# Attention of a fused attention and two-layer kernel: from half arrays to 64x64 quarters of TensorE

## The chip, the core and the metric

The kernel runs on one core of one Trainium2 chip. The metric is the device time of one launch in microseconds (us), the median of several runs; lower is better.

## What is computed

Four sequences of 768 tokens go through a retention layer of 8 heads (64 features a head) and then through two feed-forward layers:

```
state = gamma[h] * state + k_t v_t^T            # per head, 64x64
y_t   = scale * q_t state
x     = y as [3072, 512]
x     = leaky_relu(x @ w_in) @ w_out            # 512 -> 2048 -> 512, slope 0.01
out   = elu(x @ w_in2) @ w_out2                 # 512 -> 2048 -> 512
```

The weights arrive as float64 (the kernel reads their words and converts them). The retention is computed in chunks of 128 tokens: inside a chunk, scores `k q^T` are multiplied by a mask that holds the decay and the causal triangle, and the masked scores multiply `v`; a state of 64x64 for each head carries what came before from chunk to chunk.

## The kernel before, in words

There are 24 chunks of 128 tokens (6 for each sequence). `kkv[c]` holds a chunk: k and q feature-major (64 features of a head in one half of the partitions, two heads of a pair `a` one above the other), k and v token-major (128 tokens in the partitions). A chunk takes these products on TensorE (PE), all in float32, which the trace records as two instructions for each `matmul` of the program:

- scores (L240): eight products with 64 rows of contraction, 128 stationary columns and 128 moving columns. The two heads of a pair use the two halves of the rows, so two run side by side.
- inner products (L250, early L379): eight products, 128 rows of contraction (the tokens), 64 stationary columns of v, 128 moving columns of the masked scores; two halves of the columns side by side.
- state products (L254, early L360): eight, 128 rows, 64 stationary columns of k, 64 moving columns of v; two side by side. Not in the last chunk of a sequence.
- crossed products (L258, early L383): eight, 64 rows, 64 stationary columns of the state, 128 moving columns of q; all four quarters of the array side by side. Not in the first chunk of a sequence.

VectorE (DVE) multiplies the scores by the mask (L289, early L352, 128x1024), ScalarE (ACT) copies the result out, GpSimd (POOL) multiplies k and q by decay tables (`prep_k`, `prep_q`, `early_k`).

The feed-forward products are float32 split in high and low parts, 128x128 stationary and 512 moving columns: L196 and L557 in the first stage, L866, L875, L1188 and L1300 later.

Order of the work. Chunks 0 to 7 (`EC = 8`) run at the start, alone on PE, while their k, q, v and the first weights are loaded by one queue of SyncE (SP): `early_tasks` lists the order on PE by hand (`score`, `rest`, `accumulate`), and `AHEAD` says behind which chunk's load each of the first pieces of weights is loaded. The weights are converted from float64 piece by piece on DVE and ACT (L99 to L164; a piece is done when the split of L164 is), and the first step of the feed-forward layer needs piece 0. Chunks 8 to 12 are put between the steps of the feed-forward layer in `scheduled`, chunks 13 to 23 in the loop at L1345; there scores and outputs are two tasks with feed-forward products between them. The order on PE is fixed; the other engines' order is set by a planner in the program (L697 to L731, L1395 to L1437) from costs and due times that each task is given, and each engine then runs its own instructions in that order. From about chunk 13 on, DVE also makes combinations of the weights (`enc_tasks`, L974 to L988), which are stored through two buffers `fe` and one buffer `te`, and loaded again later.

In the early chunks the state of a sequence is summed in one PSUM tile `total` (tag z), and ACT copies it out scaled (`early_copy`).

Of the kernel before, what the change touches and what calls it, by code (L numbers as in the profile page):

```python
# [31 lines left out]
DM, DFF = 512, 2048  # L32
# [16 lines left out]
TABS = H + NP + EARLY + C  # L49
# [7 lines left out]
def body(ctx: ExitStack, tc: tile.TileContext, kkv, w1, w2, tabs, rows, out):  # L57
# [147 lines left out]
    with ExitStack() as actx:  # L205
# [6 lines left out]
        tab = ab.tile([P, H * C + NP * C + H + NP], F32, tag="tab", name="tab")  # L212
        mask = tab[:, : H * C].rearrange("p (r t) -> p r t", r=2)
        qtab = tab[:, H * C : H * C + NP * C]
        small = tab[:, H * C + NP * C :]
# [19 lines left out]

        def scores(c, sc):

            for a in range(NP):
                for r in range(2):
                    nc.tensor.matmul(sc[:, r, pair(a)], kv[c][half(r), 0, pair(a)], kv[c][half(r), 1, pair(a)],  # L240
                                     start=True, stop=True, skip_group_check=True)

        def outputs(c, o, t):

            cb = c % NCB
            places = [(i, k, 2 * i + k, r) for i in range(2) for k in range(2) for r in range(2)]
            by_column = [(i, k, 2 * i + k, x ^ k) for i in range(2) for k in range(2) for x in range(2)]
            for i, k, a, r in by_column:
                v = kv[c][:, 3, a * C + r * D : a * C + (r + 1) * D]
                nc.tensor.matmul(o[half(r ^ k), k, pair(i)], v, t[:, r, pair(a)], start=(i == 0), stop=True, skip_group_check=True)  # L250
            if cb < NCB - 1:
                for i, k, a, r in places:
                    hs = slice(a * C + r * D, a * C + (r + 1) * D)
                    nc.tensor.matmul(o[half(r), k, 2 * C + i * D : 2 * C + (i + 1) * D], kv[c][:, 2, hs], kv[c][:, 3, hs],  # L254
                                     start=False, stop=True, skip_group_check=True)
            if cb:
                for i, k, a, r in places:
                    nc.tensor.matmul(o[half(r ^ k), k, pair(i)], st[half(r), 2 * k + i, :], kv[c][half(r), 1, pair(a)],  # L258
                                     start=False, stop=True, skip_group_check=True)
# [19 lines left out]
        def chunk_tasks(c, task, pe_task, x_bank, t, x, needs, takes=None, uses=None, after=None):  # L279
# [8 lines left out]
            pe_task(("sc", c), 1.16, needs["sc"], lambda: scores(c, x_bank()), **more("sc"))  # L288
            task(("pt", c), "V", 1.22, [("sc", c)] + needs["pt"], lambda: nc.vector.tensor_tensor(t(), x_bank(), mask, ALU.mult), **more("pt"))  # L289
# [8 lines left out]
            pe_task(("o", c), 1.1 + (0.64 if cb < NCB - 1 else 0.0) + (0.67 if cb else 0.0), ready, lambda: outputs(c, x_bank(), t()), **more("o"))  # L298
# [12 lines left out]
        causal = early[:, EARLY : EARLY + C]  # L311
# [12 lines left out]
        total = aps.tile([P, NP, D], F32, tag="z", name="total")  # L324
# [25 lines left out]
        def early_masked(c):  # L350
            pt[c] = spare[:, :2, :] if c % 2 else ptile
            nc.vector.tensor_tensor(pt[c], scs.pop(c), mask, ALU.mult)  # L352

        def early_state(c):
            for i in range(2):
                for k in range(2):
                    for r in range(2):
                        a = 2 * i + k
                        hs = slice(a * C + r * D, a * C + (r + 1) * D)
                        nc.tensor.matmul(total[half(r), 2 * k + i, :], kv[c][:, 2, hs], kv[c][:, 3, hs],  # L360
                                         start=(c % NCB == 0 and i == k == 0), stop=True, skip_group_check=True)

        def early_copy(c):
            n = behind(c)[1]
            t = sts[(c + 1) % 2]
            if n == 0:
                nc.scalar.copy(t, total)
            else:
                for a in range(NP):
                    x = (NCB - 1) * H + (n - 1) * NP + a  # L370
                    nc.scalar.activation(t[:, a, :], total[:, a, :], AF.Copy, scale=early[:, x : x + 1])

        def early_out(c):
# [3 lines left out]
            for i, k, a, r in [(i, k, 2 * i + k, x ^ k) for i in range(2) for k in range(2) for x in range(2)]:  # L377
                v = kv[c][:, 3, a * C + r * D : a * C + (r + 1) * D]
                nc.tensor.matmul(o[half(r ^ k), k, pair(i)], v, t[:, r, pair(a)], start=(i == 0), stop=True, skip_group_check=True)  # L379

        def early_inner(c):
            for i, k, a, r in [(i, k, 2 * i + k, r) for i in range(2) for k in range(2) for r in range(2)]:
                nc.tensor.matmul(os_[c][half(r ^ k), k, pair(i)], sts[c % 2][half(r), 2 * k + i, :], kv[c][half(r), 1, pair(a)],  # L383
                                 start=False, stop=True, skip_group_check=True)
# [10 lines left out]
        def early_tasks(task, pe):  # L395
# [8 lines left out]
            def tab_load():  # L404
                nc.sync.dma_start(out=small, in_=tabs[:, : H + NP])
                nc.sync.dma_start(out=early[:, : EARLY + C], in_=tabs[:, H + NP :])
# [26 lines left out]
            def score(c):  # L433
                pe_task(("sc", c), 1.16, [loaded(c, 0), room(("pt", c))], lambda: early_score(c))
                task(("pt", c), "V", 1.22, [("sc", c), ("mask",), ("o", c - 2) if c > 1 else None], lambda: early_masked(c))
# [5 lines left out]
            def rest(c):  # L441
                with_state = c % NCB < NCB - 1
                pe_task(("o", c), 1.09, [("pt", c), room(("xlo", c))], lambda: early_out(c))
                if c % NCB:
                    pe_task(("i", c), 0.67, [("pq", c), ("stc", c - 1)], lambda: early_inner(c))
# [3 lines left out]
            def accumulate(c):  # L449
# [3 lines left out]
                pe_task(("S", c), 0.63, [("pk", c), loaded(c, 1), before], lambda: early_state(c))  # L453
# [5 lines left out]
            def mask_products():  # L459
                t = scs["mask"] = aps.tile([P, 2, BLK], F32, tag="x", name="mask")  # L460
                for r in range(2):
                    nc.tensor.matmul(t[:, r, :], few[:, r * P : (r + 1) * P], few[:, 2 * P + r * BLK : 2 * P + (r + 1) * BLK], start=True, stop=True)

            def make_mask():
                y = scs.pop("mask").rearrange("p r (a t) -> p (r a) t", a=NP)
                nc.vector.tensor_tensor(mask.rearrange("p r (a t) -> p (r a) t", a=NP), y,
                                        causal.unsqueeze(1).to_broadcast([P, H, C]), ALU.mult)
# [7 lines left out]
            task(("mask",), "V", 1.22, [("mm",), ("tab", 0)], make_mask)  # L475
# [17 lines left out]

# [948 lines left out]
def _tables():  # L1442
# [4 lines left out]
    ktab = gamma[:, None] ** (C - 1.0 - t)  # L1447
    tab = np.zeros((P, TABS), np.float32)
    tab[:, :H] = ktab.T
# [70 lines left out]
```

## Time and profile before

| what | value |
|---|---|
| median of 3 runs | 1097.19 us (1096.94 to 1097.47) |
| profiled execution, its own time | 1096.89 us |
| its span, first to last instruction | 1095.1 us |
| mean granted TensorE clock | 0.999 |
| PE busy | 99% of the span |
| DVE, ACT, POOL busy | 75%, 61%, 5% |

The profile has the busy share of every engine over the span, the groups of instructions by line, the waits, a timeline of each engine, and the chain of work that ended last. Durations are in us or ns; a matmul's end is modelled, so that neighbouring matmuls overlap in the timeline and their starts are what counts.

### The profile page before, as it was taken

To read this page: it belongs to the slowest core of one execution; us is meant where nothing else is said; L and a number is where in the kernel's file an instruction comes from. 1 tells how busy PE (TensorE), PEld (TensorE's weight loads), DVE (VectorE), ACT (ScalarE), POOL (GpSimd) and SP (SyncE) were. 2 spreads that over 40 slices of the span, in tenths; PEclk is the share of its full clock that TensorE was granted. 3 is DMA by queue.
4 is the path that set the end of the run, shared out by engine and by line. 5 is a ranking of instruction groups with operands and counts; after the bars stand their busy time and mean duration, and the time that the engine had idled before them with its cause. 6 is when DMAs were issued, how large, how long until landed. Compare 5 with 4: busy or idle time off the path is not lost.

```text
span 1095.1 us, 16119 instructions
## 1 busy us (share of the span) xinstructions
PE 1080.8 (99%) x5785; PEld 884.4 (81%) x5785; DVE 822.6 (75%) x1298; ACT 673.2 (61%) x1128; POOL 54.2 (5%) x45
## 2 busy tenths in 40 slices
PE   9999999899999999999999999999999999999998
PEld 6878877677888888888878888888888888888886
DVE  5999975885756766566675569989988989879932
ACT  4675643333656655455654478788888778878831
POOL 4110112131000000000000000000000000000000
PEclk9999999999999999999999999999999999999999
DMA  9964547999887876676867966786676776674373
GB/s 358 423 263 168 177 150 231 312 315 294 280 270 252 280 239 210 217 229 217 292 215 254 310 209 197 253 285 193 200 232 185 263 225 189 205 224 152 123 231 109
DMA packets 115592, 258.17 MB, mean 236 GB/s; under 512 B 10924, under 2 KB 41772, under 8 KB 111160
## 3 DMA queue, kind: packets, MB, share of 16 engines
q1 hardware_dynamic: 115488, 257.04, 71.4%
q8 instruction: 46, 0.75, 0.3%
q14 instruction: 34, 0.28, 0.1%
q10 hardware_dynamic: 24, 0.09, 0.0%
HBM read 200.47 MB, written 56.62 MB: 235 GB/s over the span
## 4 chain that ended last, share of the span: by engine, by line
PE 86%; DVE 6%; DMA 6%; ACT 1%; issue 0%; SPq 0%; DVEq 0%; ACTq 0%
PE y L1300 40%; PE x L1188 15%; PE h L1188 10%; PE px L1188 10%; PE y L557 4%; PE h L196 3%; DMA kv<-in_kkv 2%; DMA w1enc<-te 1%; PE y L875 1%; PE x L250 1%; DMA xscr<-xs 1%; PE x L240 1%; DMA xscr<-pt 1%; DVE te L987 1%; DMA w<-xscr 1%; PE px L866 1%
## 5 line engine op out<-in xcount | busy, mean ns | idle before, releaser
L1300 PE MATMUL y<-w,ghi 128*128 128x512 f32 x768 | 236.7, 389 | 0.0
L1300 PE MATMUL y<-ghi,w 128*128 128x512 f32 x512 | 177.1, 389 | 0.0
L1300 PEld LDWEIGHTS y<-w,ghi 128*128 128x128 f32 x768 | 144.0, 188 | 30.2 <-ACT gk L889 0.2
L1300 PE MATMUL y<-w,glo 128*128 128x512 f32 x384 | 149.4, 389 | 0.0
L1300 PEld LDWEIGHTS y<-ghi,w 128*128 128x128 f32 x512 | 96.1, 188 | 20.0
L1188 PE MATMUL x<-w 128*128 128x512 f32 x432 | 109.8, 389 | 0.1
L1300 PE MATMUL y<-glo,w 128*128 128x512 f32 x256 | 99.6, 389 | 0.0
L1320 DVE TENSOR_TENSOR glo<-gk,ghi 128x512 fp32r<-128x512 f32 x89 | 61.4, 689 | 50.6 <-ACT ghi L1317 49.8
L1188 PEld LDWEIGHTS x<-w 128*128 128x128 f32 x432 | 81.0, 188 | 17.3 <-DVE gf L1222 0.5
L1317 ACT CAST ghi<-gk 128x512 fp32r<-128x512 f32 x89 | 55.4, 622 | 52.9 <-PE y L1300 52.0
L1300 PEld LDWEIGHTS y<-w,glo 128*128 128x128 f32 x384 | 72.1, 188 | 15.0
L1222 DVE TENSOR_TENSOR gk<-gk,x 128x512 f32<-128x512 f32 x64 | 44.0, 687 | 43.4 <-PE x L1188 36.7
L1269 DVE SCALAR_TENSOR_TENSOR a<-nt,a 128x512 f32<-128x512 f32 x96 | 65.9, 686 | 11.5 <-ACT nt L1265 11.2
L1277 DVE SCALAR_TENSOR_TENSOR nt<-a,nt 128x512 f32<-128x512 f32 x96 | 66.3, 691 | 2.7
L1273 DVE SCALAR_TENSOR_TENSOR nt<-nt 128x512 f32<-128x512 f32 x96 | 65.8, 685 | 0.0
L1257 ACT ACTIVATE nt<-nt 128x512 f32<-128x512 f32 x96 | 60.8, 633 | 2.9 <-DVE gk L1281 0.4
L1261 ACT ACTIVATE a<-nt 128x512 f32<-128x512 f32 x96 | 60.8, 633 | 2.1
L1188 PE MATMUL px<-w 128*128 128x512 f32 x240 | 60.9, 389 | 0.0
L1188 PE MATMUL h<-w 128*128 128x512 f32 x240 | 60.9, 389 | 0.0
L1265 ACT ACTIVATE nt<-nt 128x512 f32<-128x512 f32 x96 | 59.5, 621 | 0.0
L1300 PEld LDWEIGHTS y<-glo,w 128*128 128x128 f32 x256 | 48.0, 188 | 10.0
L196 PE MATMUL h<-xhi,w 128*128 128x512 f32 x168 | 55.3, 394 | 0.0
(202 smaller groups left out, 2061.9 us busy)
## 6 DMA issues: line engine op xcount, KB each, us to landing
w<-w2scr SPq DMA_DIRECT2D x96, 512.0 KB, 3.9
w<-w1scr SPq DMA_DIRECT2D x168, 256.0 KB, 3.3
w<-w1enc SPq DMA_DIRECT2D x112, 256.0 KB, 3.8
kv<-in_kkv SPq DMA_DIRECT2D x22, 1024.0 KB, 7.1
raw<-in_w SPq DMA_DIRECT2D x40, 512.0 KB, 5.1
raw<-in_w SPq DMA_DIRECT2D x12, 1024.0 KB, 13.5
w2scr<-raw SPq DMA_DIRECT2D x16, 512.0 KB, 4.6
w1enc<-w SPq DMA_DIRECT2D x24, 256.0 KB, 3.9
```

Of the source, the lines that this page charges most:

```text
L196: nc.tensor.matmul(h, a, x, start=(n == 0), stop=(n == 3 * KD - 1))
L1188: nc.tensor.matmul(to, a, x, start=(first and z == 0), stop=(z == 5), skip_group_check=True)
L1222: task(("s", *hk[b]), "V", 0.7, [("c", *hk[b])] + deps, lambda: tt(at(t), at(t), bank[name], add), use=[t])
L1257: nc.scalar.activation(t, n, AF.Tanh, scale=-0.5)
L1261: nc.scalar.activation(a, t, AF.Copy, bias=-0.5, scale=0.5)
L1265: nc.scalar.activation(n, n, AF.Exp, scale=-1.0)
L1269: nc.vector.scalar_tensor_tensor(out=a, in0=n, scalar=1.0, in1=a, op0=ALU.add, op1=ALU.mult)
L1273: nc.vector.scalar_tensor_tensor(out=t, in0=n, scalar=1.0, in1=t, op0=ALU.add, op1=ALU.mult)
L1277: nc.vector.scalar_tensor_tensor(out=t, in0=a, scalar=2.0, in1=t, op0=ALU.add, op1=ALU.mult)
L1300: nc.tensor.matmul(ybank[d], a, x, start=(first and n == 0), stop=(last and n == 2))
L1317: task(hi, "A", 0.62, [made_by, last_hi[0]], lambda h=h, hi=hi: nc.scalar.copy(at(hi), at(h)), use=[h], take=("ghi", hi))
L1320: task(lo, "V", 0.7, [hi], lambda h=h, hi=hi, lo=lo: tt(at(lo), at(h), f32(at(hi)), sub), use=[h, hi], take=("glo", lo))
```

## The change

The token-major k and v are laid out anew on the host: the 128 tokens of a chunk are split in two halves of 64 (`x` = 0, 1), and a head's two halves stand below each other in the columns, in one half of the partitions (`k`, the head's pair modulo 2). All of a chunk's products now use 64x64 quarters of the array, and the four heads of `HEADS` go to the four quarters:

- Scores: 16 products in place of 8. For the first 64 keys all 128 queries are computed, for the second 64 keys only the second 64 queries: the block above the diagonal is left out. The mask and its table have 2 x 384 columns (TRI = 192 for each head) in place of 2 x 512.
- Inner products: 16, with 128 or 64 moving columns. State products: 16, 64 rows of contraction, 64 moving columns, the two halves of the tokens accumulated.
- Crossed products: each split in two of 32 stationary columns (16 in place of 8).
- Early chunks: `total` becomes two tiles, in the PSUM banks of tags h and z; ACT's unscaled copy becomes two instructions. The order on PE is new, and `AHEAD` is (3, 7, 7, 7) in place of (3, 4, 5, 7): pieces 1 to 3 of the weights are loaded after all eight chunks.
- The costs given to the planner are changed.

```diff
-        AHEAD = (3, 4, 5, 7)
+        AHEAD = (3, 7, 7, 7)
...
         def scores(c, sc):
-            for a in range(NP):
-                for r in range(2):
-                    nc.tensor.matmul(sc[:, r, pair(a)], kv[c][half(r), 0, pair(a)], kv[c][half(r), 1, pair(a)],
-                                     start=True, stop=True, skip_group_check=True)
+            for i in range(2):
+                for x in range(2):
+                    for k, r in HEADS:
+                        a = (2 * i + k) * C + x * HC
+                        nc.tensor.matmul(sc[half(k), r, cells(i, x)], kv[c][half(r), 0, a : a + HC], kv[c][half(r), 1, a : a + C - x * HC],
+                                         start=True, stop=True, skip_group_check=True)
+
+        def inner(c, o, t):
+            for i in range(2):
+                for x in range(2):
+                    for k, r in HEADS:
+                        nc.tensor.matmul(o[half(r ^ k), k, i * C + x * HC : (i + 1) * C], kv[c][half(k), 3, block(i, r, x)], t[half(k), r, cells(i, x)],
+                                         start=(i == x == 0), stop=True, skip_group_check=True)
+
+        def products(c, to, fresh):
+            for i in range(2):
+                for x in range(2):
+                    for k, r in HEADS:
+                        nc.tensor.matmul(to(k, r, i), kv[c][half(k), 2, block(i, r, x)], kv[c][half(k), 3, block(i, r, x)],
+                                         start=(fresh and i == x == 0), stop=True, skip_group_check=True)
+
+        def crossed(c, o, s, n):
+            for i in range(2):
+                for z in range(D // n):
+                    for k, r in HEADS:
+                        p = (r ^ k) * D + z * n
+                        nc.tensor.matmul(o[p : p + n, k, pair(i)], s[half(r), 2 * k + i, z * n : (z + 1) * n], kv[c][half(r), 1, pair(2 * i + k)],
+                                         start=False, stop=True, skip_group_check=True)
...
+        def masked(t, sc):
+            nc.vector.tensor_tensor(t[:, :, : 2 * TRI], sc[:, :, : 2 * TRI], mask, ALU.mult)
...
             score(0)
             for k, n in enumerate(WARM[1]):
                 pe_task(("warm", 0, k), n * 0.002, [("qtab",)], lambda n=n: warm(n))
-            rest(0)
-            for k, n in enumerate(WARM[2]):
-                pe_task(("warm", 1, k), n * 0.002, [], lambda n=n: warm(n))
             accumulate(0)
             score(1)
-            accumulate(1)
-            for c in range(1, EC):
-                if c + 1 < EC:
-                    score(c + 1)
-                rest(c)
-                if c + 1 < EC:
+            for c in range(EC):
+                if c < EC - 1:
+                    rest(c)
+                split = c + 1 < EC and (c + 1) % NCB < NCB - 1
+                if split:
                     accumulate(c + 1)
+                if c + 2 < EC and not split:
+                    score(c + 2)
+                if c == EC - 2:
+                    rest(EC - 1)
+                across(c)
+                if c + 2 < EC and split:
+                    score(c + 2)
```

`rest` now holds the inner products alone and `across` the crossed products and the copies to `xhi` and `xlo`.

## Rows read from the trace of the kernel before

**Rows 1.** The page, parts 1 and 2: busy time, and DMA in 40 slices.

```profile
PE 1080.8 (99%) x5785; PEld 884.4 (81%) x5785; DVE 822.6 (75%) x1298; ACT 673.2 (61%) x1128; POOL 54.2 (5%) x45
...
DMA  9964547999887876676867966786676776674373
```

**Rows 2.** The waits of PE, whole span: us in total, times, longest.

```profile
PE x L250 <- DVE pt L289: 4.6, 5, 2.2
PE sc L240 <- DMA kv<-in_kkv: 1.3, 2, 0.8
```

**Rows 3.** The chain that ended last: start, us, what; first and last of eleven pieces.

```profile
161.08 8.13 DMA xscr<-pt
...
234.53 1.91 DVE w L1123
```

**Rows 4.** Timeline of PE, one later chunk (97 to 106 us): start, us, instruction, count.

```profile
97.16 1.16 PE L240 MATMUL x<-kv 64*128 64x128 f32 x16
98.25 0.50 PE L196 MATMUL h<-xhi,w 128*128 128x512 f32 x1
...
102.56 1.09 PE L250 MATMUL x<-pt,kv 128*64 128x128 f32 x16
103.49 0.63 PE L254 MATMUL x<-kv 128*64 128x64 f32 x16
104.05 0.67 PE L258 MATMUL x<-kv,stg 64*64 64x128 f32 x16
104.65 0.50 PE L557 MATMUL y<-ghi,w 128*128 128x512 f32 x1
```

**Rows 5.** The same timeline, cut off at 102.84, 102.95, 103.60, 104.08 and 104.25 us.

```profile
102.56 0.55 PE L250 MATMUL x<-pt,kv 128*64 128x128 f32 x6
...
102.56 0.66 PE L250 MATMUL x<-pt,kv 128*64 128x128 f32 x8
...
103.49 0.28 PE L254 MATMUL x<-kv 128*64 128x64 f32 x4
...
104.05 0.34 PE L258 MATMUL x<-kv,stg 64*64 64x128 f32 x4
...
104.05 0.45 PE L258 MATMUL x<-kv,stg 64*64 64x128 f32 x8
```

**Rows 6.** Timeline of all engines, end of the early chunks (27 to 37 us).

```profile
28.43 1.16 PE L240 MATMUL sc<-kv 64*128 64x128 f32 x16 [0.84 <-DMA kv<-in_kkv]
...
30.77 0.28 DVE L99 TENSOR_SCALAR s<-e 128x512 uint16<-128x512 uint16 x1
30.81 1.14 POOL L348 TENSOR_TENSOR kv<-kv,early 128x512 f32<-128x512 f32 x1 [1.40 <-DMA kv<-in_kkv]
...
32.96 1.23 DVE L352 TENSOR_TENSOR early<-sc,tab 128x1024 f32<-128x1024 f32 x1
...
34.76 0.68 DVE L391 TENSOR_TENSOR xlo<-o,xhi 128x512 fp32r<-128x512 f32 x1
...
35.87 0.50 PE L196 MATMUL h<-xhi,w 128*128 128x512 f32 x1
```

**Rows 7.** Timeline of PE, scores of two early chunks that follow one another.

```profile
21.48 1.16 PE L240 MATMUL sc<-kv 64*128 64x128 f32 x16
...
24.80 1.16 PE L240 MATMUL sc<-kv 64*128 64x128 f32 x16
```

**Rows 8.** Stretches: length, busy PE, PEld, DVE, ACT, POOL, then PEclk, DMA share, GB/s.

```profile
18.00:36.00 18.00, 17.16 (x329) 14.53 (x326) 16.58 (x24) 10.15 (x26) 8.93 (x8) 1.00 1.02 421
36.00:97.00 61.00, 60.10 (x264) 49.26 (x264) 58.95 (x97) 43.12 (x61) 2.94 (x2) 1.00 0.77 301
```

**Rows 9.** Timelines of DVE and PE: a weight piece's last operation, its first use.

```profile
88.08 1.22 DVE L164 TENSOR_TENSOR w<-f,w 128x1024 fp32r<-128x1024 f32 x1
...
91.63 0.39 PE L196 MATMUL h<-xhi,w 128*128 128x512 f32 x1
```

**Rows 10.** The page, part 6: issues, KB each, median us to landing.

```profile
kv<-in_kkv SPq DMA_DIRECT2D x22, 1024.0 KB, 7.1
```

More of the change, by code (lines that the diff above doesn't have):

```diff
@@ L211, in body @@
         st, sg = stg[:, 0], stg[:, 1]
[L212 to L215, printed above, removed]
+        tab = ab.tile([P, 3 * BLK + H + NP], F32, tag="tab", name="tab")
+        mask = tab[:, : 4 * TRI].rearrange("p (r t) -> p r t", r=2)
+        qtab = tab[:, 2 * BLK : 3 * BLK]
+        small = tab[:, 3 * BLK :]
         ktab, gtab = small[:, :H], small[:, H:]
@@ L247, in outputs @@
[L247 to L250, printed above, removed]
+            inner(c, o, t)
             if cb < NCB - 1:
[L252 to L255, printed above, removed]
+                products(c, lambda k, r, i: o[half(r), k, 2 * C + i * D : 2 * C + (i + 1) * D], False)
@@ L256, in outputs @@
             if cb:
-                for i, k, a, r in places:
-                    nc.tensor.matmul(o[half(r ^ k), k, pair(i)], st[half(r), 2 * k + i, :], kv[c][half(r), 1, pair(a)],
-                                     start=False, stop=True, skip_group_check=True)
+                crossed(c, o, st, D // 2)
+        def masked(t, sc):
+            nc.vector.tensor_tensor(t[:, :, : 2 * TRI], sc[:, :, : 2 * TRI], mask, ALU.mult)
         def rows_out(c, x):
@@ L286, in more @@
                 return dict(([("use", uses[n])] if n in uses else []) + ([("take", takes[n])] if n in takes else []))
-            pe_task(("sc", c), 1.16, needs["sc"], lambda: scores(c, x_bank()), **more("sc"))
-            task(("pt", c), "V", 1.22, [("sc", c)] + needs["pt"], lambda: nc.vector.tensor_tensor(t(), x_bank(), mask, ALU.mult), **more("pt"))
+            pe_task(("sc", c), 0.93, needs["sc"], lambda: scores(c, x_bank()), **more("sc"))
+            task(("pt", c), "V", 0.95, [("sc", c)] + needs["pt"], lambda: masked(t(), x_bank()), **more("pt"))
             ready = [("pt", c)]
@@ L297, in chunk_tasks @@
             yield
[L298 removed]
+            pe_task(("o", c), 0.88 + (0.5 if cb < NCB - 1 else 0.0) + (0.67 if cb else 0.0), ready, lambda: outputs(c, x_bank(), t()), **more("o"))
             task(("xs", c), "A", 0.6, [("o", c)] + needs["xs"], lambda: rows_copy(x_bank(), x()), **more("xs"))
@@ L351, in early_masked @@
             pt[c] = spare[:, :2, :] if c % 2 else ptile
-            nc.vector.tensor_tensor(pt[c], scs.pop(c), mask, ALU.mult)
+            masked(pt[c], scs.pop(c))
         def early_state(c):
[L355 to L361, printed above, removed]
+            if not totals:
+                totals.extend(pool.tile([P, 2, D], F32, tag=tag, name="total") for pool, tag in ((ps, "h"), (aps, "z")))
+            products(c, lambda k, r, i: totals[k][half(r), i, :], c % NCB == 0)
         def early_copy(c):
@@ L366, in early_copy @@
             if n == 0:
-                nc.scalar.copy(t, total)
+                for k in range(2):
+                    nc.scalar.copy(t[:, 2 * k : 2 * k + 2, :], totals[k])
             else:
@@ L376, in early_out @@
             o = os_[c] = pool.tile([P, 2, BLK], F32, tag=tag, name="o")
-            for i, k, a, r in [(i, k, 2 * i + k, x ^ k) for i in range(2) for k in range(2) for x in range(2)]:
-                v = kv[c][:, 3, a * C + r * D : a * C + (r + 1) * D]
-                nc.tensor.matmul(o[half(r ^ k), k, pair(i)], v, t[:, r, pair(a)], start=(i == 0), stop=True, skip_group_check=True)
+            inner(c, o, t)
         def early_inner(c):
-            for i, k, a, r in [(i, k, 2 * i + k, r) for i in range(2) for k in range(2) for r in range(2)]:
-                nc.tensor.matmul(os_[c][half(r ^ k), k, pair(i)], sts[c % 2][half(r), 2 * k + i, :], kv[c][half(r), 1, pair(a)],
-                                 start=False, stop=True, skip_group_check=True)
+            crossed(c, os_[c], sts[c % 2], D // 2)
         def early_x(c, low):
```

62 lines of the change are left out of this document (38 added, 24 removed).

## The prediction

> **What bounds the kernel now.** I read the busy shares first: PE is busy for 99% of the span [rows 1]. As ends of matmuls are modelled, that alone proves little, so the waits came next. PE waits for little: 4.6 us for the masked scores of five later chunks and 1.3 us for the loads of early ones [rows 2]. So PE's own instructions set the time nearly everywhere, and a microsecond taken off them is a microsecond gained, with two exceptions. At the start the DMA engines are full (421 GB/s at a share of 1.02) and chunk 6's scores wait for their load [rows 8, 6]. And between 161 and 235 us the eleven pieces that the chain of waits prints are all transfers or DVE work [rows 3], in slices where DMA is at 0.8 and more [rows 1].
>
> **How a round is priced.** Cutting the timeline off shows how products side by side advance. Inner products: from the 6th to the 8th instruction 0.11 us [rows 5], so a round of two tiles with 128 moving columns takes 0.11. Crossed products, four tiles: also 0.11 from 4 to 8 [rows 5]. State products, two tiles with 64 columns: from 4 instructions at 0.28 to 16 at 0.63 six rounds, 0.058 each [rows 5, 4]. So a round costs its moving columns, not the number of tiles in it. What a group takes beyond its rounds is the change of tile shape: from state to crossed products 0.56 - 8 x 0.058 = 0.10, from crossed products to the next layer 0.60 - 4 x 0.11 = 0.16, and between inner and state products, of one shape, 0.93 - 8 x 0.11 = 0.05 [rows 4]. I take 0.15 for a change of shape.
>
> **The change on PE, per chunk.** Each product is two instructions, four tiles a round.
> - Scores: 32 instructions, in 4 rounds of 128 columns and 4 of 64. Before 8 x 0.11 = 0.88, after 4 x 0.11 + 4 x 0.058 = 0.67: 0.21 less.
> - Inner products: the same sum, 0.21 less.
> - State products: 32 instructions in 8 rounds of 64 columns, as many as before: nothing. No row shows four tiles with 64 columns. The ends are 0.058 a round (two tiles, 64 columns) and 0.11 (four tiles, 128 columns), the second 8 x 0.05 = 0.42 dearer. I take 0.058, since four tiles cost no more than two at 128 columns.
> - Crossed products: 32 instructions of 32 columns. If eight tiles run in a round there are still 4 rounds; if four do, there are 8, 0.44 more. Starts of four tiles fall within 0.03 us [rows 5], so eight need about 0.06 of the 0.11 that a round lasts. I take 4 rounds and 0.03 for the later last start, and keep 0.44 as the other end.
> - Changes of shape: a later chunk has five, before (in and out for the scores, three for the outputs) and after (the 32-column tiles are a shape of their own). The step from 64x64 to 64x32 shows nowhere; the ends are 0 and 0.16, and I take the 0.15 of the others.
>
> On the last point the Trainium skill, "TensorEngine Tiling (Array Packing)", Key Properties, says that changing the tiling mode drains TensorE. The gaps of 0.10 and 0.16 against 0.05 agree.
>
> **Later chunks, 8 to 23.** 16 x 0.42 = 6.7 us less, 14 x 0.03 = 0.4 more for the crossed products (two of these chunks have none): 6.3. Not all arrives. Eight of these chunks lie where transfers and DVE set the pace, 8 x 0.4 = 3.2 us. The mask there costs 0.95 rather than 1.23 (768 columns, between 0.68 for 512 and 1.23 for 1024 [rows 6]), but DVE stands in order behind stores of weight combinations, which do not change. Between nothing and all lost I take half: 1.6. Sum 4.7.
>
> **Early chunks, 0 to 7.** Two chunks' scores are 3.32 us apart [rows 7]. After: 0.42 less, 0.03 more, and two changes of shape instead of four (inner, state products and scores now share one), 0.30 less: 2.63. A chunk's load is 1.05 MB [rows 10], 2.5 us at 421 GB/s [rows 8]. So the loads, which before made PE wait, now nearly keep pace with PE. Moving two half-megabyte pieces of weights behind chunk 7 brings that chunk 1.05 MB earlier: 30.8 [rows 6] - 2.5 = 28.3 us. From there the new order needs scores 0.9, chunk 6's inner products 0.8, state products 0.6, chunk 7's inner products 0.8, a change of shape and crossed products 0.7: 3.8. The mask (0.95 plus handover) fits behind the middle two, POOL's product with k (1.14 [rows 6]) behind the scores. PE may be some tenths late, so the feed-forward layer starts at 32.4 instead of 35.87: 3.5 us. At the very start the first state products wait for POOL, but the loads have to come anyway. ACT's second copy and the two-part mask table lie beside this.
>
> Does the layer behind keep up? DVE, converting weights, is busy 58.95 of 61 us from 36 to 97 [rows 8]. The tightest use is a piece done at 89.3 and used at 91.63 [rows 9]: 2.3 us of slack. Piece 1 before had its first DVE operation at 30.77, with a mask and three `xlo` (3.3 us) of attention still behind it [rows 6]. After, it lands 1.2 us behind chunk 7, at 29.5, and can begin about 30.2 with some 2.2 us left: 1.7 us ahead. With 2.3 that covers 3.5, just. If not, the gain falls to 2.3; if the loads were no longer the limit it could be 4.
>
> **Sum.** Against the profiled execution's 1096.9: - 4.7 - 3.5 = 1088.7. The runs' median is 0.3 higher; I say 1089.
>
> **Rivals.**
> 1. A round costs about 0.11 whatever its columns, because four tiles have to be loaded with weights and started. For: no row has four tiles with 64 columns. Against: four start within 0.03 us, and two at 64 columns take 0.058. Then scores and inner products gain nothing, 13 later chunks' state products cost 0.42 more and the crossed products 0.4 in all: + 5.8; early, 0.45 more and 0.30 less leave the start about where it is. 1103, slower. It decides from about 0.08 a round, where the gain and the loss of a chunk meet.
>
> The Trainium skill, "TensorE: Matmul & The Clock Gate", "Wait — 56ns, not 53.3ns?", gives such a rule: starts are never closer than about 25 ns. Estimated by that page, each group of 32 instructions would take 0.8 us, later chunks 6.8 us more, 1104. Four starts in 0.03 us [rows 5] contradict it for tiles side by side.
>
> 2. The 32-column tiles run only four at a time: 14 x 0.41 = 5.8 us back, and early chunks 3.05 apart lose about 2.5 of the 3.5. With nothing else lost: 1095.5 or a little below. For: no such tile in the trace; against: nothing but the pattern of the others.
> 3. The rest swallows more: the whole 3.2 us between 161 and 235, and the early gain down to 1 to 2 because weights come too late. 1092 to 1094. For: DVE and DMA are full there; against: the slack counted above.
> 4. The planner, given new costs, orders DVE worse and the waits of [rows 2] double: 1093. Or better, and 2 to 4 us of them go: 1085.
>
> **Chances.** Forecast with its spread (1084 to 1091.5) 0.70; rival 1 0.06; rival 2 0.09; rival 3 and the bad side of 4 0.15. The range runs from 1083.5 (nothing lost, waits shortened, no extra change of shape: 1088.7 - 1.6 - 1.4 - 2) to 1094.5; left out are rival 1, most of rival 2 and the far tails. A difference of 0.2%, 2.2 us, is about what a measurement of this kernel can tell from none. Faster by more (below 1095) is 0.70 + 0.15 + little of rival 2: 0.87; the same 0.06; slower 0.07.
>
> **What would show it.** Scores and inner products should last about 0.9 each in the timeline instead of 1.16 and 1.09, state products stay near 0.65, crossed products near 0.7. The first feed-forward product should start near 32.4 us. PE should not wait for weights between 36 and 97 us, and its waits for masked scores should stay near 4 to 6 us in all. State products of 1 us or crossed products of 1.1 would prove rival 1 or 2; a first feed-forward product at 34 or later, or waits of several us at L196, would show the early gain gone.

## The result and the profile after

The changed kernel is slower. Its median is 1108.26 us (1107.25 to 1110.3, 4 runs) against 1097.33 us (1096.94 to 1098.4) for the kernel before: ratio 1.010, 95% interval 1.0083 to 1.0118. The forecast was 1089.0 with a range to 1094.5 and 0.07 for slower. The profiled execution took 1107.25 us with a span of 1105.4, 10.4 us more than that of the kernel before (1096.89).

PE does less work and takes longer. From the page of the changed kernel, its first line and parts 1 to 3 (against [rows 1]):

```profile
span 1105.4 us, 18941 instructions
...
PE 1074.4 (97%) x7193; PEld 878.5 (79%) x7193; DVE 816.3 (74%) x1299; ACT 673.1 (61%) x1130; POOL 52.8 (5%) x45
...
PE   7899999888999999999999999999999999999998
...
q8 instruction: 57, 0.93, 0.3%
```

The slices of PE in the kernel before, page part 2:

```profile
PE   9999999899999999999999999999999999999998
```

PE's busy time falls from 1080.8 to 1074.4 us, 6.4 less, and its idle time grows by about 17. The two slices that lost most are the first and the second (7 and 8 tenths; 9 and 9 before), so the place to look is the first 50 us. The last line of the first block is the queue that brings instructions: 57 packets of 16 KB.

The timeline of PE, one later chunk (columns: start, us, instruction, count; it answers to [rows 4]):

```profile
108.59 0.90 PE L253 MATMUL x<-kv 64*64 64x128 f32 x32
109.42 0.50 PE L198 MATMUL h<-xhi,w 128*128 128x512 f32 x1
...
112.36 0.90 PE L260 MATMUL x<-pt,kv 64*64 64x128 f32 x32
113.08 0.65 PE L267 MATMUL x<-kv 64*64 64x64 f32 x32
113.66 0.67 PE L275 MATMUL x<-kv,stg 64*32 64x128 f32 x32
114.25 0.50 PE L584 MATMUL y<-ghi,w 128*128 128x512 f32 x1
```

This is what the forecast said of the array. Scores take 0.90 (1.16 before), inner products 0.90 (1.09), state products 0.65 (0.63), crossed products 0.67 (0.67). From the start of one group to the next, scores hold PE for 0.83, crossed products in tiles of 32 columns for 0.59: all eight tiles run in one round. State products, 32 instructions in 8 rounds, are followed after 0.58. Before, the four groups held PE for 1.09, 0.93, 0.56 and 0.60 [rows 4], so a later chunk now takes 0.46 us less of PE where the forecast had 0.39. Over the 16 later chunks that is 7.2 us of PE's busy time (225.16 to 217.93 between the two marks set below), where 6.3 was forecast.

The loss stands in the early chunks. The timeline of PE there:

```profile
22.55 0.43 PE L260 MATMUL o<-pt,kv 64*64 64x128 f32 x8 [3.13 <-issue]
22.72 0.28 PE L267 MATMUL total<-kv 64*64 64x64 f32 x3
22.81 0.22 PE L260 MATMUL o<-pt,kv 64*64 64x64 f32 x2
22.83 0.27 PE L267 MATMUL total<-kv 64*64 64x64 f32 x2
22.87 0.22 PE L260 MATMUL o<-pt,kv 64*64 64x64 f32 x2
22.88 0.68 PE L267 MATMUL total<-kv 64*64 64x64 f32 x27
23.49 1.06 PE L275 MATMUL o<-kv,stg 64*32 64x128 f32 x32
24.48 1.56 PE L253 MATMUL sc<-kv 64*64 64x128 f32 x32
25.81 1.27 PE L260 MATMUL o<-early,kv 64*64 64x128 f32 x19
28.66 0.44 PE L260 MATMUL o<-early,kv 64*64 64x128 f32 x8 [1.58 <-issue]
...
34.77 0.69 PE L260 MATMUL o<-pt,kv 64*64 64x128 f32 x8 [3.13 <-issue]
...
40.71 0.70 PE L267 MATMUL total<-kv 64*64 64x64 f32 x15 [0.71 <-issue]
...
47.13 0.50 PE L198 MATMUL h<-xhi,w 128*128 128x512 f32 x1
```

The first feed-forward product starts at 47.13 us; it was 35.87 [rows 6], and 32.4 was forecast. Three things are to be read here. First, PE stops in the middle of a group of like products whose operands are all there, and the releaser is "issue": it waits for nothing that the profile shows. Second, the starts after a stop lie 6.11, 6.11 and 5.94 us apart. Third, between 22.55 and 28.66 stand 8+3+2+2+2+27+32+32+19 = 127 products; each has its weight load, which makes 254 instructions. The stretches from 28.66 to 34.77 and from 34.77 to 40.71 hold 127 as well. With PE's semaphore instructions, which the page doesn't count as busy, the blocks between the stops hold exactly 256. So PE stops where another 256 instructions are used up.

The waits of PE over the whole span (us in total, times, longest), against [rows 2]:

```profile
PE o L260 <- issue: 9.0, 4, 3.1
PE x L253 <- DVE stg L301: 4.3, 3, 1.7
PE x L260 <- DVE pt L288: 3.3, 4, 1.5
PE x L253 <- DVE stg L303: 2.9, 1, 2.9
```

Beside the stops there is a second loss: in the later chunks PE waits 10.5 us for DVE (the last three rows), where before it was 4.6 for the masked scores [rows 2] and 0.2 for a state.

Stretches of the changed kernel (length, busy PE, PEld, DVE, ACT, POOL, then PEclk, DMA share, GB/s), against [rows 8]:

```profile
24.00:27.00 3.00, 3.00 (x75) 2.30 (x58) 1.13 (x2) 2.14 (x6) 0.85 (x1) 0.50 1.01 418
27.00:33.80 6.80, 3.06 (x128) 2.48 (x127) 4.08 (x6) 1.44 (x4) 3.00 (x4) 1.00 1.02 415
33.80:44.00 10.20, 8.51 (x214) 7.32 (x218) 2.38 (x5) 2.66 (x7) 1.14 (x1) 0.50 0.85 352
```

The granted clock is 0.50, the 1.2 GHz level, in two stretches that begin during or just behind stops of 3.13 us; before, it was 1.00 there [rows 8]. The DMA engines are full until about 42 us (a share of 0.96 from 40 to 42, of 0.17 from 42 to 44), and no stop comes after that.

I split the time at two marks: the first feed-forward product, and the first product of the next stage (L1188 before, L1215 after):

| kernel | first mark | second mark | between |
|---|---|---|---|
| before | 35.87 | 266.82 | 230.95 |
| after | 47.13 | 276.66 | 229.53 |

So 11.3 us are lost ahead of the first mark, and of the 7.2 us that the array saves between the marks only 1.4 arrive; PE's waits for DVE there grow by 5.9. The work after the second mark differs by about half a microsecond.

### The profile page after: what moved, and what is told of

Read it like the earlier page. It is cut to its first block, busy times and chain, and to the rows that moved or that the text cites. A ratio compares the mean times of both kernels' runs of the same rounds, so it can differ in the third digit from the quotient of the medians.

```text
span 1105.4 us, 18941 instructions
## 1 busy us (share of the span) xinstructions
PE 1074.4 (97%) x7193; PEld 878.5 (79%) x7193; DVE 816.3 (74%) x1299; ACT 673.1 (61%) x1130; POOL 52.8 (5%) x45
## 4 chain that ended last, share of the span: by engine, by line
PE 86%; DVE 7%; DMA 5%; issue 1%; ACT 0%; SPq 0%; DVEq 0%; ACTq 0%
PE y L1327 38%; PE x L1215 14%; PE px L1215 9%; PE h L1215 9%; PE y L584 4%; PE h L198 3%; PE y L902 1%; DMA xscr<-xs 1%; DMA w1enc<-fe 1%; DMA kv<-in_kkv 1%; PE x L260 1%; PE h L893 1%; PE px L893 1%; DMA w1enc<-te 1%; PE sc L253 1%
## 5 line engine op out<-in xcount | busy, mean ns | idle before, releaser
L1215 PE MATMUL x<-w 128*128 128x512 f32 x432 | 109.8, 389 | 0.1
L1347 DVE TENSOR_TENSOR glo<-gk,ghi 128x512 fp32r<-128x512 f32 x89 | 61.3, 689 | 53.7 <-ACT ghi L1344 53.0
L1215 PEld LDWEIGHTS x<-w 128*128 128x128 f32 x432 | 81.0, 188 | 17.3 <-DVE gf L1249 0.5
L1296 DVE SCALAR_TENSOR_TENSOR a<-nt,a 128x512 f32<-128x512 f32 x96 | 65.9, 686 | 11.3 <-ACT nt L1292 11.0
L1215 PE MATMUL h<-w 128*128 128x512 f32 x240 | 60.9, 389 | 0.0
L1215 PE MATMUL px<-w 128*128 128x512 f32 x240 | 60.9, 389 | 0.0
```

The lines of the kernel that those rows point to most:

```text
L1215: nc.tensor.matmul(to, a, x, start=(first and z == 0), stop=(z == 5), skip_group_check=True)
L1296: nc.vector.scalar_tensor_tensor(out=a, in0=n, scalar=1.0, in1=a, op0=ALU.add, op1=ALU.mult)
L1347: task(lo, "V", 0.7, [hi], lambda h=h, hi=hi, lo=lo: tt(at(lo), at(h), f32(at(hi)), sub), use=[h, hi], take=("glo", lo))
```

## Theories and experiments

**Supply**: PE's own instructions come too slowly while DMA is full. An early chunk had 64 products and as many weight loads, 128 instructions; the change makes it 256, and a block of 256 takes about 6.1 us to come. Two rivals: **order**, that the new sequence of early steps makes PE late; and **clock**, that the half clock is the cause and not a consequence. For the later chunks: DVE stands behind the stores of weight combinations (the **buffers** that they leave free, and the landing time, **lag**, that the planner gives them).

All times are device us. "Marks" are the two of the table above, each from one profiled execution; single executions of the kernel before spread from 1094.91 to 1100.3 in one session, so the marks of one profile are good to some 2 us and verdicts rest on the medians. The first three kernels ran once each; they are read from their traces, not from their times.

| kernel | median (runs) | kernel before beside it | ratio, 95% | marks | between |
|---|---|---|---|---|---|
| x1_before_more_instr | 1104.7 (1) | 1097.06 | | 40.27, 274.69 | 234.42 |
| x2_after_old_order | 1111.08 (1) | 1097.06 | | 48.93, 280.66 | 231.73 |
| x4_after_quiet_dma | 1112.23 (1) | 1097.06 | | | |
| x5_hybrid | 1096.98 (10) | 1097.06 | 1.0006, 0.9989 to 1.0024 | 36.87, 268.01 | 231.14 |
| z_before_buffers | 1094.11 (7) | 1097.56 | 0.9967, 0.9952 to 0.9982 | 35.01, 265.10 | 230.09 |
| z_hybrid_buffers | 1090.82 (4) | 1097.56 | 0.9935, 0.9920 to 0.9949 | 36.15, 260.24 | 224.09 |
| y_before_lag | 1099.37 (10) | 1097.56 | 1.0015, 1.0005 to 1.0025 | 35.24, 269.82 | 234.58 |
| y_hybrid_lag | 1090.91 (4) | 1097.56 | 0.9940, 0.9917 to 0.9962 | 36.56, 259.38 | 222.82 |
| w_after_buffers | 1102.32 (2) | 1097.20 | 1.0054, 1.0033 to 1.0076 | 49.51, 273.69 | 224.18 |
| w_before_ahead | 1098.35 (10) | 1097.20 | 1.0014, 1.0004 to 1.0025 | 37.23, 269.88 | 232.65 |
| w_hybrid_buf_lag | 1088.12 (4) | 1097.20 | 0.9923, 0.9907 to 0.9940 | 35.90, 258.22 | 222.32 |
| w_hybrid_buf_lag_ahead | 1087.40 (4) | 1097.20 | 0.9921, 0.9906 to 0.9937 | 36.47, 256.75 | 220.28 |

### More instructions in the kernel before

Early inner products are cut in halves of 64 columns and crossed products in tiles of 32, each twice as many. Order and scores stay.

```diff
-            for i, k, a, r in [(i, k, 2 * i + k, x ^ k) for i in range(2) for k in range(2) for x in range(2)]:
-                v = kv[c][:, 3, a * C + r * D : a * C + (r + 1) * D]
-                nc.tensor.matmul(o[half(r ^ k), k, pair(i)], v, t[:, r, pair(a)], start=(i == 0), stop=True, skip_group_check=True)
+            for i, k, n in [(i, k, n) for i in range(2) for k in range(2) for n in range(2)]:
+                for x in range(2):
+                    a, r = 2 * i + k, x ^ k
...
+                    nc.tensor.matmul(o[half(r ^ k), k, i * C + n * D : i * C + (n + 1) * D], v, t[:, r, a * C + n * D : a * C + (n + 1) * D],
+                                     start=(i == 0 and n == 0), stop=True, skip_group_check=True)
```

> The kernel before with the early chunks' inner products cut in two of 64 moving columns and their crossed products in two of 32 stationary columns: 16 more products for most of the chunks 0 to 7, the same columns streamed, the same order and loads. Theory 'supply' (PE's instructions come in blocks of 16 KB, and while the loads fill the DMA engines a block takes about 6.1 us, as the changed kernel's stops at every 256th instruction show): an early chunk then has some 192 PE instructions in place of 128, 4.6 us at that pace where it took 3.3, so PE stops inside groups for a reason that the profile calls issue, and the first feed-forward product starts at 43 to 46 us instead of 35.9; the run is 7 to 10 us slower than before. Theory 'order' (the new order on PE and the new places of the weight loads delay the start): nothing changes but some tenths, first feed-forward product at 36 to 37 us. Theory 'clock' (PE fell to half clock first, and the stops follow from that): as with order, since nothing here idles PE.

The feed-forward layer starts at 40.27 instead of 35.87. The timeline of PE in this kernel:

```profile
18.18 0.33 PE L381 MATMUL o<-pt,kv 128*64 128x64 f32 x3
19.85 1.09 PE L381 MATMUL o<-pt,kv 128*64 128x64 f32 x29 [1.34 <-issue]
20.86 0.67 PE L387 MATMUL o<-kv,stg 64*32 64x128 f32 x32
21.46 0.69 PE L360 MATMUL total<-kv 128*64 128x64 f32 x16
22.07 1.16 PE L240 MATMUL sc<-kv 64*128 64x128 f32 x16
23.17 1.15 PE L381 MATMUL o<-early,kv 128*64 128x64 f32 x32
24.25 0.40 PE L387 MATMUL o<-kv,early 64*32 64x128 f32 x2
25.75 0.66 PE L387 MATMUL o<-kv,early 64*32 64x128 f32 x30 [1.09 <-issue]
```

The kernel before has no such stop; with more instructions they appear, again 5.90 us apart (then 6.05 and 5.85: the next starts are 31.80, where a wait for DVE falls on the same place, and 37.65) and again after 29+32+16+16+32+2 = 127 products, in whichever group the count falls (here first in inner, then in crossed products). Order and clock cannot explain this: the order is the old one, and no half clock was granted ahead of the first mark (1.00 in every stretch). Supply was right in kind and too high in size: a chunk here has 96 products, so at 5.9 us for 127 it takes 4.5 instead of 3.32 us [rows 7], and the supply limits the four chunks between the stops from 19.85 to 37.65, not all eight: 4 x 1.2 = 4.7, measured 4.4. Another 3.5 us were lost between the marks, where the code is the same: PE waited 2.0 us more for DVE, once for 3.48, and behind that wait the clock was at 0.50, the 1.2 GHz level, from 212.0 to 215.4 us, which shows as 1.6 us more busy time. Why DVE was later there was not tried.

### The change with the order of before

```diff
-        AHEAD = (3, 7, 7, 7)
+        AHEAD = (3, 4, 5, 7)
...
-            for c in range(EC):
-                if c < EC - 1:
-                    rest(c)
...
+            for c in range(1, EC):
+                if c + 1 < EC:
+                    score(c + 1)
+                rest(c)
                 across(c)
+                if c + 1 < EC:
+                    accumulate(c + 1)
```

> The changed kernel with the early chunks in the order of before and with the weight pieces loaded behind chunks 3, 4, 5 and 7 as before. Theory 'supply': the early chunks have as many PE instructions as in the changed kernel, so the stops stay, and the first feed-forward product starts at 45 to 49 us (47.1 in the changed kernel); the time stays within 2 us of it. Theory 'order': the start comes back to 36 us or earlier and the time to 1090 to 1097. Theory 'clock': in between, as the old order has the warm-up matmuls in the old place.

The first mark stands at 48.93, later still, and the stops are there: 6.6 us ahead of inner and 2.9 ahead of crossed products, with the starts after them at 23.16, 30.14, 36.15 and 42.08, one block of 6.98 us and two of about 6. The longest stop, in the timeline of PE:

```profile
30.14 0.56 PE L260 MATMUL o<-early,kv 64*64 64x128 f32 x14 [4.01 <-issue]
```

The order is not the cause.

### The change without the loads of chunks 2 to 7

The chunks read the tiles of chunks 0 and 1. The pieces of weights, meant to come behind chunk 7, came at once instead, since their queue waits for tiles alone. So DMA was full until about 28 us and idle after: not what was meant, but it gives both conditions in one run.

```diff
-            kv[c] = wp.tile([P, 4, DM], F32, tag=f"w{MF - 1 - c}", name="kv")
+            kv[c] = kv[c % 2] if c > 1 else wp.tile([P, 4, DM], F32, tag=f"w{MF - 1 - c}", name="kv")
...
-                chain.append((("kv", c, 0), 2.5, lambda c=c: whole(c)))
+                chain.append((("kv", c, 0), 2.5, lambda: None))
```

> The changed kernel, whose chunks 2 to 7 load nothing and use the tiles of chunks 0 and 1 again, and whose weight pieces are loaded only after the early chunks; this leaves out the loads of six chunks, and the whole run is longer because the weights come late. Only the early chunks are read. Theory 'supply': with the DMA engines idle a block of instructions should come in 2 to 3.5 us rather than 6.1, the stops of 3.1 us shrink to under 1 us each or vanish, and the last early crossed product ends at 30 to 35 us (47.2 in the changed kernel). If a block takes 6 us whatever the load on DMA, the stops stay at about 3 us and the end near 45. Theory 'order': the stops stay, since the order is that of the changed kernel.

Stretches of this kernel (columns as above), then the timeline of PE:

```profile
24.00:27.00 3.00, 2.87 (x80) 2.37 (x83) 0.00 (x0) 0.00 (x0) 0.00 (x0) 0.50 0.98 415
27.00:30.00 3.00, 2.46 (x51) 2.06 (x52) 1.52 (x2) 1.42 (x5) 1.27 (x1) 0.50 0.40 161
30.00:33.00 3.00, 2.75 (x81) 2.25 (x80) 0.03 (x1) 0.00 (x0) 0.00 (x0) 0.50 0.07 25
...
36.00:40.00 4.00, 3.98 (x189) 3.47 (x193) 1.65 (x2) 1.26 (x5) 1.69 (x2) 1.00 0.02 4
```

```profile
24.13 0.69 PE L260 MATMUL o<-pt,kv 64*64 64x128 f32 x8 [3.03 <-issue]
...
30.25 0.70 PE L260 MATMUL o<-early,kv 64*64 64x128 f32 x9 [0.79 <-issue]
...
34.07 0.84 PE L260 MATMUL o<-pt,kv 64*64 64x128 f32 x32
...
38.16 0.65 PE L267 MATMUL total<-kv 64*64 64x64 f32 x32
...
41.62 0.46 PE L267 MATMUL total<-kv 64*64 64x64 f32 x15 [0.44 <-issue]
```

The starts after the stops are 18.11, 24.13 and 30.25, 6.0 and 6.1 apart; the last of these blocks began while DMA was full. Once it is idle, the next two ends of 127 products fall inside the groups at 34.07 and 38.16, and neither shows a stop. The third, at 41.62, shows 0.44, after 3.3 us. So the slow supply belongs to the full DMA engines. The half clock outlasts the stops here (0.50 at 30 to 33 us, with PE busy 2.75 of 3.00), and the block that begins there at 30.25 ends without a stop, so it is not what made PE stop. The last early crossed product ended at 43.5 us, where 30 to 35 was expected, since DMA was full for longer than meant. The total says nothing of the early part, as the weights came in another order: PE stood 4.8 us for the first converted piece.

### Old early chunks, new later chunks

Chunks 0 to 7 as before, 8 to 23 in quarters; the shorter mask of the later ones comes as a table of 0.4 MB.

```diff
-            scores(c, scs[c])
+            scores0(c, scs[c])
...
-            masked(pt[c], scs.pop(c))
+            nc.vector.tensor_tensor(pt[c], scs.pop(c), mask0, ALU.mult)
...
-            inner(c, o, t)
+            for i, k, a, r in [(i, k, 2 * i + k, x ^ k) for i in range(2) for k in range(2) for x in range(2)]:
```

> Chunks 0 to 7 as in the kernel before (layout, forms, order, loads), chunks 8 to 23 in quarters as in the changed kernel; the second mask comes as a table of 0.4 MB. Theory 'supply': the early chunks end as before, first feed-forward product at 35.9 us, no stops; the later chunks keep PE's saving of 0.4 us a chunk, of which 1.4 to 4.7 us arrive (1.4 in the changed kernel): 1092 to 1096 in all, faster than both. Theories 'order' and 'clock' expect the same of the early part; a first feed-forward product later than 38 us would speak against all three.

No difference: 1.0006 (0.9989 to 1.0024). The early loss is gone, and so are the stops. (The first mark is at 36.87, 1.0 later than before. The new table has no part in that, as its load is issued at 45.5 us; PE waited 2.3 us for early loads instead of 1.3.) But the forecast's gain does not arrive. Waits of this kernel, PE over the whole span, then DVE from 97 to 280 us:

```profile
PE x L254 <- DVE stg L311: 3.6, 1, 3.6
PE x L254 <- DVE stg L309: 2.9, 3, 1.7
PE x L268 <- DVE pt L296: 2.8, 3, 1.5
```

```profile
DVE fe L1012 <- DMA w1enc<-fe: 16.1, 6, 5.2
```

The last line's counterpart in the kernel before, same stretch:

```profile
DVE fe L974 <- DMA w1enc<-fe: 8.8, 4, 3.2
```

PE waits 9.3 us for DVE's masks and states. DVE in turn waits 16.1 us to write a combination of weights (`fe`) into a buffer that a store to HBM still reads; in the kernel before that was 8.8 us. The chunk that PE finishes sooner finds DVE standing in line behind the store. The clock was lower too: behind waits of 1.74 and 3.60 us this execution was at 0.50, the 1.2 GHz level, from 184.6 to 188.0 and from 225.5 to 228.9 us, and PE's busy time between the marks fell by 4.1 us only (225.16 to 221.03), where the changed kernel's fell by 7.2.

### More buffers for the stores

Four more `fe` and one more `te`, in memory that the raw weights of the encoding held before and take over later.

```diff
-        stock["cf"] += [lazy(lambda: cv.tile([P, W], U32, tag="f", name="raw2")) for _ in range(2)]
...
+        stock["ef"] += two(lazy(lambda: cv.tile([P, 2, BLK], F32, tag="f", name="fe2")))
+        stock["pf"] = [..., lazy(lambda: cv.tile([P, 4, QB], F32, tag="f", name="te2"))]
...
+        turns_into["encs",] += [("cf", lazy(lambda: cv.tile([P, W], U32, tag="f", name="raw2"))) for _ in range(2)]
```

> The kernel before with four buffers fe and two te for the weight combinations in place of two and one (the extra ones are the two tiles f, which the next stage gets when the combinations are done). Theory 'stores' (between 160 and 280 us DVE stands behind the stores of weight combinations for a buffer, and masks and states of the chunks, behind it in order, come late to PE): DVE's waits for w1enc stores fall from 11 us to under 4, PE's waits for L289 from 4.6 to under 2, and the time to 1093 to 1096. Rival 'pace' (the loads and row stores, on full DMA engines, set the time of that stretch): the waits move to other transfers, 1096 to 1099.

> The same buffers in the hybrid (chunks 0 to 7 as before, 8 to 23 in quarters). Theory 'stores': the saving of quarters in the later chunks, 6.3 us of PE, now arrives: PE's waits for masks and states fall from 9.3 us to under 4 and the time to 1088 to 1092, 4 to 6 us faster than the kernel before with these buffers. Theory 'pace': no faster than 1095, and within 1.5 us of the kernel before with these buffers.

> The changed kernel with four buffers fe and two te. If the loss at the start (instruction supply) and the loss between 160 and 280 us (stores) are two separate things, the first stays whole, first feed-forward product at 46 to 49 us, and the second goes: PE's waits for masks and states fall from 10.5 to under 5 us, the time from 1108 to 1101 to 1104. If the late waits only mirror the late start, the time stays at 1106 to 1109.

The kernel before gains 0.33%, the hybrid 0.65%: 1094.11 against 1090.82 us, so with buffers the later chunks in quarters are worth 3.3 us, and between the marks 230.09 - 224.09 = 6.0 of the 7.4 that PE's busy time falls (225.19 to 217.80). Their waits: DVE of the hybrid, 97 to 280 us, and PE, whole span:

```profile
DVE fe L1013 <- DMA w1enc<-fe: 1.0, 1, 1.0
```

```profile
PE x L268 <- DVE pt L296: 3.5, 4, 1.3
...
PE x L254 <- DVE stg L309: 1.0, 1, 1.0
...
PE x L254 <- DVE stg L311: 0.9, 1, 0.9
```

DVE's 16.1 us have become 1.0, PE's 9.3 have become 5.4, and the clock stays at 1.00 between the marks. So buffers did not only end the stores' part of the waits, they also gave back 3.2 us of busy time (221.03 to 217.80). More waiting is left than was expected (5.4 us where under 4 was, and 3.1 for masks in the kernel before where under 2 was). Of the 6.0 us, 1.1 go to the later first mark (36.15 against 35.01) and 0.8 are lost behind the second.

With the same buffers the whole change stands at 1102.32 us, ratio 1.0054: its second loss is mended (224.18 us between the marks, as in the hybrid) and its first is whole (first mark 49.51, stops of 10.6 us at L260 and L267). This parts the two losses.

### A truer landing time for the planner

The planner takes 2.5 us for a store's landing; set to 5.5, it puts the next use of the buffer later.

```diff
-                    use=[key], lag=2.5)
+                    use=[key], lag=5.5)
```

> The kernel before, the planner told that a store of weight combinations takes 5.5 us to land rather than 2.5 (5.1 measured). Theory 'stores': DVE's own order then has masks and states ahead of operations that wait for a store; PE's waits for L289 fall below 3 us, 1094 to 1096. Theory 'pace': 1096 to 1099.

> The same landing time for the planner in the hybrid. Theory 'stores': PE's waits for masks and states fall from 9.3 us to under 6, 1091 to 1095. Theory 'pace': 1095 to 1098.

In the hybrid this does as much as the buffers (0.9940; 222.82 us between the marks). In the kernel before, where a gain was expected, it costs 0.15%: DVE's wait for `fe` falls from 8.8 to 3.2 us, but its wait for ACT's `xs` rises from 5.8 to 16.3. A wait has only changed its place there. What the planner would need to know of ACT was not tried.

### Loads ahead of weights, and the best version

The change also moved two pieces of weights behind chunk 7. That alone, in the kernel before, and then all that helped together:

```diff
-        AHEAD = (3, 4, 5, 7)
+        AHEAD = (3, 7, 7, 7)
```

> The kernel before with AHEAD = (3, 7, 7, 7) alone: pieces 1 to 3 of the weights behind all eight chunks. By the prediction's working chunk 7 lands 2.5 us earlier, at 28.3 us; PE, which needs 3.3 us a chunk, then loses only its waits for loads, 1 to 1.5 us: 1095 to 1097, no waits for weights at L196. Rival 'order' (this move is what delays the changed kernel): first feed-forward product later than 37 us, slower than 1099.

> The hybrid with both the buffers and the landing time of 5.5 us in the planner. Both act on the same waits, so the gains (6.7 us each) do not add: 1087 to 1091, waits for masks and states under 4 us. If they acted on different ones: 1083 to 1086.

> The same with AHEAD = (3, 7, 7, 7): PE's waits for early loads (about 1.5 us) go, 1086 to 1090. If the weights come too late instead, PE waits at L198 and the time is 1090 to 1093.

Earlier loads alone bring nothing, where 1095 to 1097 was expected: 1.0014, first mark 37.23 instead of 35.87 in an execution of 1100.6. PE's wait for loads falls from 1.3 to 0.7 us, and a new one takes its place, 1.2 us for a mask at L379 and 0.5 for one ahead of the scores. Buffers and landing time together give 1088.12 us; with the moved loads 1087.40, which is no clear difference from that. Both beat the kernel before by about 0.8% and the changed one by some 20 us.

## Why the prediction was wrong

**The step that failed** is "Early chunks, 0 to 7": from 3.32 us between two chunks' scores it took off array time and changes of shape, "After: 0.42 less, 0.03 more, and two changes of shape instead of four [...] 2.63", checked this against the loads ("now nearly keep pace with PE") and the other engines, and put the feed-forward layer at 32.4 us. It never counted PE's instructions as something that has to be brought. They double, from 128 to 256 a chunk. The runs put in its place: four blocks of 127 products, from 16.42 to 40.71 us, at 6.07 us each, instead of four chunks at 2.63: 4 x 3.44 = 13.8 of the 14.7 us between 32.4 and 47.13. No rival named it, so the range missed it too. The kernel before shows no trace of it because its early chunk uses 128 instructions in 3.32 us, 256 in 6.6, just slower than the 6.1 in which they come.

**The half clock** was not foreseen, and by the order in time it is a consequence (x1 stops without it): from 28.66 to 34.77 PE ran at full clock and stopped 3.13 us, from 34.77 to 40.71 it ran at half clock and stopped 0.71, and both blocks took 6 us. It fills the stop. What it costs after 40.71, where no stop is left, was only read from rows (scores 1.56 instead of 0.90, crossed products 1.10 instead of 0.67), not taken away by a run.

**Later chunks: right in kind, too small.** "Between nothing and all lost I take half: 1.6", of 3.2. Lost were 7.2 - 1.4 = 5.8, and x5_hybrid's median confirms that nearly nothing is left. The mechanism was named ("DVE stands in order behind stores of weight combinations"), and the buffers show it: with them 6.0 of 7.4 arrive. But I bounded the loss by the eight chunks where the old trace shows DVE and transfers in the chain [rows 3]; a faster PE makes DVE late in chunks that the old chain does not show. The forecast also read DMA "at 0.8 and more" over all of that stretch; the slice from 164 to 192 us reads 7 [rows 1], and the trace gives 0.72 there.

**Loads moved forward** were to give part of the early 3.5 us. Alone they give nothing measurable (w_before_ahead). That the loads bound the early chunks was read from a wait of 1.3 us [rows 2]; a mask is as late as they are.

**Right** were the prices of the array: 0.90 for scores and inner products, state products near 0.65, crossed products near 0.7, eight tiles in a round. That refutes rival 1 (a round of 0.11 whatever its columns) and rival 2 (four tiles of 32 columns at a time). The mask at 768 columns took 0.96 us, 0.95 forecast. The array saves somewhat more than was counted in the later chunks, 7.2 us rather than 6.3: scores gave 0.26 each where 0.21 was counted, and the 32-column tiles cost nothing (0.60 before and after). The 6.4 us that PE's busy time fell in all is near 6.3 by luck, since the half clock lengthens the early products. By its time rival 1 came nearest (1103), by luck, as its mechanism did not happen. In kind it was rival 3: it had the whole 3.2 us and part of the early gain lost, but no early loss. Rival 4's bad side, waits of [rows 2] doubled, is there (10.5 us). Buffers take about half of it away, and in the hybrid a truer landing time in the plan does as much, so stores and plan are not parted here. The signs that I named did their work: "a first feed-forward product at 34 or later" was one.

## What to carry to other kernels

Small tiles that run side by side cost the array next to nothing here and the instruction supply a lot: before cutting products finer, count instructions per microsecond in each stretch, and be wary where DMA is full. A stop with the releaser "issue" in the middle of a group of like instructions, again and again after the same count, is the sign. And when an engine gets faster, look at who hands it its work in order: the gain goes first into that engine's own waits, and here a few spare buffers brought it out.

## What was not expected of the hardware

**Instructions share the DMA engines.** The changed kernel has 18941 - 16119 = 2822 instructions more than the kernel before, 11 x 256 and 6, and the instruction queue carries 57 - 46 = 11 packets more of 16 KB. The hybrid, with 1888 more (7.4 x 256), has 53 packets, 7 more; the kernel with 448 more (1.75 x 256) has 48, 2 more. The line of the kernel before, page part 3:

```profile
q8 instruction: 46, 0.75, 0.3%
```

By their number all of the queue's packets are PE's. Its matmuls, weight loads and semaphore instructions make 46.4 blocks of 256 in the kernel before, 57.4 in the changed one, 53.7 in the hybrid and 48.1 in x1; the queue has 46, 57, 53 and 48 packets. Counted so, the stops of the changed kernel, of x1, of x2 and of x4 all stand behind PE's 449th instruction or a multiple of 256 later.

So small a share, 0.3%, hid it: what counts is how long one packet's instructions take to arrive when the queues are full, about 6 us for 256 in the changed kernel, in x1, x2 (once 6.98) and x4, against 3.3 us with DMA idle. The DMA records of the traces hold each packet, and they show where the time goes (us):

| kernel, DMA | PE begins a block | next packet starts | is in | PE begins the next block |
|---|---|---|---|---|
| after, full | 22.55 | 26.33 | 27.26 | 28.66 |
| after, full | 28.66 | 32.47 | 33.39 | 34.77 |
| x1, full | 25.75 | 29.50 | 30.46 | 31.80 |
| x2, full | 23.16 | 27.89 | 28.84 | 30.14 |
| x4, full | 18.11 | 21.86 | 22.82 | 24.13 |
| x4, idle | 38.36 | 39.07 | 40.28 | 41.62 |
| before, full | 29.52 | 33.02 | 33.94 | 35.66 |

At every stop of these four kernels PE goes on 1.3 to 1.6 us after the packet is in (in x1 at 31.80 too, which the waits put down to DVE). The packet itself takes no longer when DMA is full (0.9 us, against 1.1 to 1.4). What grows is the time before it starts: 3.1 to 4.7 us behind PE's start on the block, against 0.7 in the idle row. Whether the packet stands behind the loads or is asked for later, the records do not show. The last row is the kernel before: PE reached its next block 1.7 us after the packet was in, a few tenths from a stop.

The Trainium skill, "Runtime: NRT & Kernel Launch", Instruction fetch mechanics, says that an engine's instructions come in blocks of 16 KiB, 256 of them, the next block while the current one runs, and that this is mostly hidden. The counts here agree with the block; the stops of 3.13 us show that it is not hidden where products are short and DMA is full, and the packet for the next block starts while the current one runs, as the page has it.

**Starts of small tiles.** In the later chunk 32 state products are done 0.58 us after they began, 0.018 us each on average. The Trainium skill, "TensorE: Matmul & The Clock Gate", Wait — 56ns, not 53.3ns?, would have had them no closer than about 25 ns; for tiles side by side this trace disagrees, as the prediction held.
